# Two attention layers on one core: in the first layer, the fourth row block's transposes one unit later, the double work and its loads moved by up to three units

## The chip, the cores and the metric

The kernel runs on one core of a Trainium2 chip. A core has a matmul engine (TensorE, PE in the profile; its weight loads are PEld), three engines for elementwise work (VectorE or DVE, ScalarE or ACT, GpSimd or POOL) and SyncE (SP), which here issues nearly all DMA transfers. Each engine runs its own instructions in the order in which they were written, and waits at an instruction until what it needs is there. The metric is the time of one execution on the device in microseconds. Before the change it is 3582.98 us, the median of three runs (3582.79 to 3584.32).

## The reference

The input is one sequence of 2048 rows of width 640. Two kinds of block alternate, and the pair runs twice with the same weights:

```python
x = x + A(layernorm(x))   # attention, 32 heads of 20
x = x + B(layernorm(x))   # dense 640 -> 1536 -> 640 with relu squared
x = x + A(layernorm(x))
x = x + B(layernorm(x))

# A:
qkv = x @ wqkv                      # (2048, 640) @ (640, 1920)
p = softmax(q @ k.T * 20 ** -0.5)   # per head, over all 2048 keys
out = (p @ v) @ wo
# B:
r = max(x @ w1 + b1, 0)
out = (r * r) @ w2 + b2
```

Everything is float32. The kernel splits each operand of the projections into a high and a low part of the matmul's float32r format and adds three products, so that little precision is lost.

## The kernel before

**Stages.** A layer (`layer`) is a projection stage (`qkv`), an attention stage (`attention`), and an output and dense stage. The first layer's projection stage takes the first 340 us or so. Only this stage is touched.

**Rows and preparation.** The 2048 rows are four row blocks, `tb` 0 to 3, of 512 rows. Before a block can be projected, the generator `front` has to load its four row tiles, take their statistics (DVE, lines 244 and 245, and two small POOL operations), normalise them (DVE, line 252), transpose them on PE (line 469, in two groups of 12 and 8) and evict the result in high and low parts into five tiles `xnT`. For blocks 2 and 3 the eviction is a copy (ACT, L263), a rounding cast (ACT, L264) and a subtraction (POOL, L271). A `yield` ends each piece; `wait` holds two numbers of empty pieces, one ahead of the statistics, one ahead of the transposes. `fronts` chains the generators of blocks 1 to 3; `begin_first` builds them.

**Units.** The queries and keys are ten column groups of 128, `pos` 0 to 9. A unit is one column group for one row block: 15 matmuls of 512 columns into one PSUM bank. The list `UNITS` has 40: units 0 to 15 take the first four column groups (`FIRST`) block by block, units 16 to 39 the other six, four blocks each. Units 8 to 11 belong to block 2, units 12 to 15 to block 3. From unit 4 on, a matmul runs as two halves of 64 rows (L356 and L368), the second 19 matmuls behind the first (`LAG`). After each unit its bank is evicted and the result stored to DRAM; a store is issued some 16 steps after the unit's end. Sixteen value units (`v_unit`) follow the 40.

**Maxima.** Softmax needs the largest score of each query. The stage finds a part of them beside the projections, because DVE is the slowest at it. A *double* handles two chunks of 512 keys, `c` and `c + 1`, in one item: `step_two` multiplies the queries with the difference of the chunks (`kd`, tile "d" or "e") and ACT takes its Relu (L695); `both_two` multiplies them with chunk `c`, and DVE adds the two and takes the maximum (L702). Both matmuls are at L662. An item such as `(0, 0, "d")` (head group 0, query block 0) has eight pairs, that is 16 calls; the stage has 24 items, 384 calls. `tiles` loads what an item needs, if it isn't there: keys, difference keys and queries, six transfers each. When an item begins, the tiles of the next two are asked for as well.

**Order.** `between` is called after every matmul of a unit. It subtracts the matmul's cost (1, in a value unit 0.65) from a pace; when the pace is used up, it makes one call of the double work and adds 1.94. It issues stores that are due. Every third call in the first layer advances the preparation by one piece (`next(rest)`). `LATE_STEPS` says after which unit of the first layer tiles are loaded and doubles released. Calls that are left when the value units are over are made in a row:

```python
        while double or twos or begun:
            some()
```

**Buffers.** `xnT`, evicted units, weights, keys and queries share 42 slots of SBUF; row tiles and scratch tiles share 11; transposes and doubles take turns in five PSUM banks (`ps_q`), the units in three (`ps_pj`).

Of the kernel before, what the change touches and what calls it, by code (L numbers as in the profile page):

```python
# [39 lines left out]
def tile_layers(  # L40
# [26 lines left out]
    def slot(shape, dtype, label):  # L67
        return arena.tile(shape, dtype, tag="slot", name=name(label))

    def dma(eng, dst, src):  # L70

        if dst.dtype == F32R:
            dst = dst.bitcast(F32)
        if src.dtype == F32R:
            src = src.bitcast(F32)
        eng.dma_start(dst, src)  # L76
# [17 lines left out]
    ps_q = Ring(0, 1, 2, 3, 4)  # L94
# [20 lines left out]
    x_in = a_x[0]  # L115
# [92 lines left out]
    def raw_cols(src, j):  # L208
        raw = xtile("raw")
        dma(nc.sync, raw.rearrange("p (k m) -> p k m", k=KD),  # L210
            src[:, j * P : (j + 1) * P].rearrange("(k p) m -> p k m", p=P),
        )
        return raw
# [25 lines left out]
    def stats(x):  # L239

        st = small.tile([P, 2, 6], F32, tag="bst", bufs=3, name=name("bst"))
        mv = small.tile([P, 2], F32, tag="mv", bufs=6, name=name("mv"))
        for i in range(2):
            nc.vector.bn_stats(st[:, i, :], x[:, i * HALF : (i + 1) * HALF])
        nc.vector.bn_aggr(mv, st)
        var = mv[:, 1:2]
        nc.gpsimd.tensor_tensor(var, var, eps_t, op=ALU.add)
        nc.gpsimd.tensor_tensor(var, var, half_t, op=ALU.pow)
        return mv

    def normalise(eng, x, mv):
        eng.tensor_scalar(x, x, mv[:, 0:1], mv[:, 1:2], op0=ALU.subtract, op1=ALU.mult)  # L252

    def split_to(dst_hi, dst_lo, src):

        nc.scalar.copy(dst_hi, src)
        nc.vector.tensor_sub(dst_lo, src, dst_hi.bitcast(F32))  # L257

    def split_on_pool(dst_hi, dst_lo, src, r=None, hi=None):

        if r is None:
            r = xtile("r")[:, :QB]
        nc.scalar.copy(r, src)  # L263
        (hi or pool_hi)(dst_hi, r)  # L264
        pool_lo(dst_lo, r, dst_hi.bitcast(F32))
# [59 lines left out]
    def row_tile(src, r):  # L325
        t = xtile("x")
        dma(nc.sync, t, src[r * P : (r + 1) * P, :])
        return t
# [120 lines left out]
    def front(tb, x_src, bank, wait=(1, 1)):  # L449

        rows = [row_tile(x_src, tb * 4 + i) for i in range(4)]
        for _ in range(wait[0]):
            yield
        mvs = []
        for x in rows:
            mvs.append(stats(x))
            yield
        yield
        for x, mv in zip(rows, mvs):
            normalise(nc.vector, x, mv)  # L460
            yield
        for _ in range(wait[1]):
            yield
        res = []
        for ks in (range(3), range(3, KD)):
            dsts = [bank("xt") for _ in ks]
            for k, dst in zip(ks, dsts):
                for i in range(4):
                    nc.tensor.transpose(  # L469
                        dst[:, i * P : (i + 1) * P], rows[i][:, k * P : (k + 1) * P], ident  # L470
                    )
            for k, dst in zip(ks, dsts):
                t = slot([P, 2, QB], F32R, "xnT")
                if tb > 1:
                    split_on_pool(t[:, 0, :], t[:, 1, :], dst, None, nc.scalar.copy)
                else:
                    split_to(t[:, 0, :], t[:, 1, :], dst)
                res.append(t)
            if len(res) == KD:
                xt_[tb] = res  # L480
            yield
# [6 lines left out]
    def first_front(x_src):  # L488


        rows = [row_tile(x_src, i) for i in range(4)]
        yield
        mvs, dsts = [], [ps_all("xt") for _ in range(KD)]

        def turn(i):
            normalise(nc.vector, rows[i], mvs[i])
            for k in range(KD):
                nc.tensor.transpose(
                    dsts[k][:, i * P : (i + 1) * P], rows[i][:, k * P : (k + 1) * P], ident
                )  # L500
            warm(6 if i == 3 else 3)

        warm(11)
        for i in range(4):
            mvs.append(stats(rows[i]))
            if i:
                turn(i - 1)
            yield
        turn(3)
        yield  # L510
        res = []
        for dst in dsts:
            t = slot([P, 2, QB], F32R, "xnT")
            split_to(t[:, 0, :], t[:, 1, :], dst)
            res.append(t)
            if len(res) == KD:
                xt_[0] = res
            yield

    def fronts(steps):  # L520


        for n, f in enumerate(steps):
            for m, _ in enumerate(f):
                if m == 8 and n + 1 < len(steps):
                    next(steps[n + 1])
                yield
# [311 lines left out]
    def prep_job():  # L839
# [44 lines left out]
        19: [("double", 3)],  # L884
    }
    LATE_STEPS = {
        3: [("tiles", (0, 0, 0))],
        9: [("tiles", (0, 0, "d"))],
        11: [("double", 0), ("tiles", (1, 0, "d"))],
        13: [("double", 1)],  # L890
        16: [("double", 2)],
        19: [("double", 3)],
    }
# [507 lines left out]
    def begin_first():  # L1401
        f = first_front(x_in)
        next(f)
        for pos in range(FIRST):
            raws.append(raw_cols(wqkv, ORDER[pos]))
        for p in range(2):
            dma(nc.sync, d_one[:, p, :], ones)
        steps = [front(tb, x_in, ps_q, (4, 2)) for tb in (1, 2, 3)]
        for _ in range(5):
            next(f)  # L1410
        for pos in range(2):
            w_qk.put(
                raws.pop(0), pos * 10, pos * 10 + KD, KD, nc.scalar.copy,
                nc.vector.tensor_sub if pos else pool_lo,
            )
        next(steps[0])
        yield from f
        w_qk.put(raws.pop(0), 20, 20 + KD, KD, nc.scalar.copy, pool_lo)
        yield from fronts(steps)

    ones = slot([2, QB], F32, "ones")
    nc.vector.memset(ones, 1.0)
    ahead = second()
    layer(True, x_in, d_x[0], d_x[1], begin_first(), ahead)
    layer(False, d_x[1], d_x[2], x_out, ahead, None)

# [27 lines left out]
```

## Time and profile before

| | |
|---|---|
| median of three runs | 3582.98 us |
| profiled execution | 3582.95 us, its span 3581.2 us |
| mean granted PE clock | 0.998 |
| first projection stage | 0 to about 340 us |
| second projection stage | about 1800 to 2118 us |
| DMA over the span | 121 GB/s |

The profile lists the busy time of each engine, what each engine waited for, and the granted clock of PE, where 1.00 is full speed. Its lines start with a time in microseconds from the start of the span and a length. A bracket at the end is the idle time of the engine ahead of the instruction, with what ended it. A busy PE isn't PE at its peak: an instruction that is stretched by a lower clock counts as busy.

### The profile page before, as it was taken

The page shows a single profiled execution, that of the slowest core. Times are in us where ns is not written, and L with a number is a line of the kernel's source. Part 1 is how long each engine was busy: PE and PEld are TensorE (multiplying, and loading weights), DVE is VectorE, ACT ScalarE, POOL GpSimd, SP SyncE. Part 2 cuts the span into 40 slices and gives each one's busy share as a digit, 9 for nine tenths or more (in the row PEclk, how much of TensorE's full clock was granted, in tenths as well). Part 3 has the DMA queues.
Part 4 walks back from the last instruction along what each step waited for, and adds up shares of the span by engine and source line. Part 5 has one row for each costly group of instructions (what it writes and reads, how often), then busy time and mean ns, then how long its engine had stood idle before and what let it go on. Part 6 is the DMA issues. An engine that isn't in the chain of part 4 may idle for free.

```text
span 3581.2 us, 70902 instructions
## 1 busy us (share of the span) xinstructions
PE 3558.4 (99%) x25544; PEld 2153.0 (60%) x25544; DVE 2630.3 (73%) x5078; ACT 2708.6 (76%) x4730; POOL 832.4 (23%) x939
## 2 busy tenths in 40 slices
PE   9999999999999999999999999999999999999999
PEld 7998333333333336988989973333333333378998
DVE  6999888888888881444579988888888888725443
ACT  5888999999999995122238889999999999932221
POOL 5430334322112211112243201212112211201110
PEclk9999999999999999999999999999999999999999
DMA  7666455422222136722356652222232121375221
GB/s 239 220 219 193 136 161 153 148 73 70 59 56 57 47 106 199 259 74 74 103 190 223 197 176 67 79 73 60 69 84 57 42 60 51 108 239 208 75 81 37
DMA packets 281598, 431.87 MB, mean 121 GB/s; under 512 B 70948, under 2 KB 130084, under 8 KB 281248
## 3 DMA queue, kind: packets, MB, share of 16 engines
q1 hardware_dynamic: 280720, 425.64, 38.2%
q8 instruction: 203, 3.33, 0.4%
q10 hardware_dynamic: 528, 1.70, 0.2%
q14 instruction: 147, 1.20, 0.1%
HBM read 282.52 MB, written 144.68 MB: 119 GB/s over the span
## 4 chain that ended last, share of the span: by engine, by line
PE 94%; DVE 2%; ACT 1%; DMA 1%; issue 1%; POOL 1%; SPq 0%; ACTq 0%; POOLq 0%; DVEq 0%
PE banks L771 27%; PE banks L336 21%; PE banks L756 18%; PE banks L662 17%; PE banks L368 5%; PE banks L356 5%; PE banks L351 1%; ACT e L766 0%; PE banks L469 0%; DMA x<-d_x 0%; SPq L76 0%; DVE h L257 0%; DVE r L1302 0%; ACT r L1301 0%; DVE x L252 0%
## 5 line engine op out<-in xcount | busy, mean ns | idle before, releaser
L766 ACT ACTIVATE e<-banks 128x512 f32<-128x512 f32 (+1 forms) x3416 | 2037.7, 690 | 52.9 <-PE banks L756 12.7
L673 DVE TENSOR_REDUCE mx<-banks 128x1 f32<-128x512 f32 x2560 | 1620.3, 685 | 323.1 <-PE banks L662 275.4
L771 PE MATMUL banks<-e,vg 128*32 128x512 f32 x8192 | 1094.3, 605 | 2.3 <-ACT e L766 2.3
L662 PE MATMUL banks<-k,q 60*128 60x512 f32 x3360 | 1056.5, 411 | 0.5 <-DVE mx L702 0.4
L756 PE MATMUL banks<-q,k 62*128 62x512 f32 x4096 | 1049.9, 442 | 1.0
L756 PEld LDWEIGHTS banks<-q,k 62*128 62x128 f32 x4096 | 515.7, 185 | 751.3 <-ACT e L766 494.0
L662 PEld LDWEIGHTS banks<-k,q 60*128 60x128 f32 x3360 | 564.9, 185 | 196.6 <-ACT e L766 65.0
L702 DVE CUSTOM_DVE_ANT_0 rl<-banks,rl 128x512 f32<-128x512 f32 x736 | 476.5, 689 | 52.0 <-PE banks L662 28.8
L695 ACT ACTIVATE rl<-banks 128x512 f32<-128x512 f32 x736 | 399.1, 601 | 58.5 <-PE banks L662 49.5
L771 PEld LDWEIGHTS banks<-e,vg 128*32 128x32 f32 x8192 | 162.2, 108 | 353.7 <-issue 269.3
L1301 ACT ACTIVATE r<-banks,b_t 128x512 f32<-128x512 f32 x96 | 66.2, 689 | 377.9 <-PE banks L336 227.3
L336 PE MATMUL banks<-w,h 128*128 128x320 f32 x2304 | 348.9, 310 | 2.7 <-DVE h L257 2.5
L336 PEld LDWEIGHTS banks<-w,h 128*128 128x128 f32 x2304 | 339.2, 188 | 11.4 <-DVE h L257 6.4
L336 PE MATMUL banks<-xnT,w 128*128 128x512 f32 x1440 | 329.7, 389 | 0.0
L368 PE MATMUL banks<-xnT,wqk 64*128 64x512 f32 x1080 | 326.1, 393 | 0.0
L356 PE MATMUL banks<-xnT,wqk 64*128 64x512 f32 x1080 | 325.6, 394 | 0.0
L336 PEld LDWEIGHTS banks<-xnT,w 128*128 128x128 f32 x1440 | 269.5, 188 | 55.3
L815 POOL TENSOR_TENSOR few<-few,minus_t 128x16 f32<-128x16 f32 x62 | 179.9, 2902 | 228.9 <-DMA few<-d_s 228.8
L662 PE MATMUL banks<-kd,q 60*128 60x512 f32 x736 | 208.3, 399 | 2.8 <-ACT rl L695 2.4
L268 POOL CAST mr<-nt 128x32 fp32r<-128x32 f32 x64 | 13.5, 211 | 835.8 <-DVE nt L728 835.8
L356 PEld LDWEIGHTS banks<-xnT,wqk 64*128 64x128 f32 x1080 | 199.7, 187 | 11.4 <-issue 2.0
L368 PEld LDWEIGHTS banks<-xnT,wqk 64*128 64x128 f32 x1080 | 201.5, 187 | 7.6
(93 smaller groups left out, 2731.7 us busy)
## 6 DMA issues: line engine op xcount, KB each, us to landing
q<-d_qk SPq DMA_DIRECT2D x876, 80.0 KB
d_qk<-ev SPq DMA_DIRECT2D x80, 512.0 KB
k<-d_qk SPq DMA_DIRECT2D x444, 80.0 KB
x<-d_x SPq DMA_DIRECT2D x96, 320.0 KB
d_o<-ot SPq DMA_DIRECT2D x248, 80.0 KB
ot<-d_o SPq DMA_DIRECT2D x38, 512.0 KB
d_v<-v SPq DMA_DIRECT2D x32, 512.0 KB
vg<-d_v SPq DMA_DIRECT2D x32, 512.0 KB
```

Source lines behind the costliest of these rows:

```text
L336: nc.tensor.matmul(dst, a, b, start=(n == 0), stop=(n == last))
L356: top = nc.tensor.matmul(dst, a[:64], b[:64], start=start, stop=last)
L368: low = nc.tensor.matmul(dst, a, b, start=False, stop=last, skip_group_check=True)
L662: nc.tensor.matmul(dst, q_t[t][b : b + 60, p, sub * P : (sub + 1) * P], k_t[t // NQB, c][b : b + 60, p, :], start=True, stop=True,)
L673: nc.vector.tensor_reduce(maxima(t)[:, 2 * p + par, sub, c : c + 1], dst, axis=AX.X, op=ALU.max)
L695: nc.scalar.activation(r, dst, AF.Relu)
L702: nc.vector.tensor_tensor_reduce(out=r[par], in0=dst, in1=r[par], scale=1.0, scalar=LEAST, op0=ALU.add, op1=ALU.max, accum_out=maxima(t)[: ...
L756: nc.tensor.matmul(dst, k_t[t // NQB, kt // 4][b : b + 62, p, (kt % 4) * P : (kt % 4 + 1) * P], q_t[t][b : b + 62, p, :], start=True, stop ...
L766: nc.scalar.activation(dst, src, AF.Exp, scale=SCALE)
L771: nc.tensor.matmul(acc[32 * h : 32 * h + 32, :], v_t[t // NQB, kt // 8][:, kt % 8, 32 * h : 32 * h + 32], es[p][:, par, :], start=(kt == 0 ...
L815: nc.gpsimd.tensor_tensor(few, few, minus_t, op=ALU.pow)
L1301: nc.scalar.activation(r, dst, AF.Relu, bias=b1_t[:, f : f + 1])
```

## The change

Three places change, all for the first layer's projection stage.

- `front` of block 3 gets seven empty pieces ahead of its transposes in place of two. Five pieces are 15 calls of `between`, one unit.
- The keys of chunk 0 and the queries of item (0, 0) are loaded after unit 6, not after unit 3; the difference keys of group 0 after unit 8, not after unit 9.
- The first two doubles are released after unit 10, not 11, together with the loads of group 1's first item; the next four after unit 12, not 13. The later releases, after units 16 and 19, stay.

```diff
     LATE_STEPS = {
-        3: [("tiles", (0, 0, 0))],
-        9: [("tiles", (0, 0, "d"))],
-        11: [("double", 0), ("tiles", (1, 0, "d"))],
-        13: [("double", 1)],
+        6: [("tiles", (0, 0, 0))],
+        8: [("tiles", (0, 0, "d"))],
+        10: [("double", 0), ("tiles", (1, 0, "d"))],
+        12: [("double", 1)],
         16: [("double", 2)],
         19: [("double", 3)],
     }
...
-        steps = [front(tb, x_in, ps_q, (4, 2)) for tb in (1, 2, 3)]
+        steps = [front(tb, x_in, ps_q, (4, 7 if tb == 3 else 2)) for tb in (1, 2, 3)]
```

## The prediction

> **What bounds the kernel now.** I read the page first, then the waits of the matmul engine (PE) alone, then stretches of time, then the order of work inside the two stretches that fell short.
>
> ```profile
> span 3581.2 us, 70902 instructions
> PE 3558.4 (99%) x25544; PEld 2153.0 (60%) x25544; DVE 2630.3 (73%) x5078; ACT 2708.6 (76%) x4730; POOL 832.4 (23%) x939
> ```
>
> PE idles 22.8 us in all, so a change of order can win only there, or where PE is busy at half clock. The waits (total, times, longest) name the place:
>
> ```profile
> PE banks L469 <- DVE x L252: 5.0, 4, 2.9
> PE banks L662 <- ACT rl L695: 2.4, 8, 0.4
> PE banks L662 <- DVE mx L702: 0.4, 1, 0.4
> ```
>
> L469 is the transposes of a row block, L252 the normalising in front of them. The stretches around the longest wait (busy us of PE, PEld, DVE, ACT, POOL; then the granted clock, DMA share, GB/s):
>
> ```profile
> 54.00:56.00 2.00, 0.33 (x1) 0.14 (x1) 2.00 (x3) 0.00 (x0) 2.00 (x2) 1.00 0.00 0
> 56.00:58.00 2.00, 0.88 (x3) 0.59 (x4) 1.61 (x3) 0.00 (x0) 0.67 (x1) 0.64 0.94 358
> 58.00:60.00 2.00, 2.00 (x11) 1.67 (x11) 0.00 (x0) 1.78 (x4) 0.53 (x1) 0.50 0.81 261
> 62.00:64.00 2.00, 2.00 (x12) 1.59 (x12) 0.00 (x0) 1.48 (x3) 1.41 (x2) 0.65 1.09 254
> ```
>
> PE starves from 52 to 57 us and is then granted half its clock until about 63.4 (0.65 is 1.4 us at a half and 0.6 at full). The order inside, start and length in us:
>
> ```profile
> 38.29 1.53 PE L469 MATMUL banks<-ident,x 128*128 128x128 f32 x12
> 40.65 1.09 PE L469 MATMUL banks<-ident,x 128*128 128x128 f32 x8
> 45.20 0.39 PE L356 MATMUL banks<-xnT,wqk 64*128 64x512 f32 x1
> ...
> 51.78 0.39 PE L356 MATMUL banks<-xnT,wqk 64*128 64x512 f32 x1
> 52.34 0.33 PE L469 MATMUL banks<-ident,x 128*128 128x128 f32 x1 [0.18 <-DVE x L252]
> 55.60 0.33 PE L469 MATMUL banks<-ident,x 128*128 128x128 f32 x1 [2.93 <-DVE x L252]
> 57.07 2.70 PE L469 MATMUL banks<-ident,x 128*128 128x128 f32 x10 [1.14 <-DVE x L252]
> 61.28 1.97 PE L469 MATMUL banks<-ident,x 128*128 128x128 f32 x8
> 71.81 0.41 PE L662 MATMUL banks<-kd,q 60*128 60x512 f32 x2
> ```
>
> The first two rows are the third block's 12 and 8 transposes, unhindered. The next two are 29 steps apart, so a projection step takes 0.227 us. The fourth block's transposes follow: one, a gap, one, a gap, ten, and eight from 61.28 on. The last row is the first double.
>
> **What the change moves.** Every projection step calls the pacing function once, every third call advances the preparation, a unit has 15 steps. Five more waiting turns are 15 steps: the fourth block's transposes go from steps 141 and 144 to 156 and 159, one unit or 15 x 0.227 = 3.4 us of other matmuls. Nothing ahead of them on VectorE (DVE), ScalarE (ACT) or GpSimd (POOL) moves.
>
> **Idle before the transposes.** What DVE and POOL do meanwhile:
>
> ```profile
> L252 DVE TENSOR_SCALAR x<-x,mv x4: 559/1076/1553, 51.7 to 56.9; 128x640 f32<-128x640 f32 x4
> 53.99 3.55 DVE L252 TENSOR_SCALAR x<-x,mv 128x640 f32<-128x640 f32 x3
> 53.73 2.94 POOL L271 TENSOR_TENSOR ev<-r,ev 128x512 fp32r<-128x512 f32 x2
> 49.70 1.30 POOL L271 TENSOR_TENSOR ev<-r,ev 128x512 fp32r<-128x512 f32 x1
> 51.81 0.59 ACT L263 COPY r<-banks 128x512 f32<-128x512 f32 x1 [2.16 <-POOL mv L248]
> 52.43 0.62 ACT L264 CAST ev<-r 128x512 fp32r<-128x512 f32 x1
> ```
>
> A normalising takes 0.56 us alone and 1.55 us beside a POOL subtraction. The rows' tiles are ready at 52.3, 55.5, 57.0 and 57.5. With the change PE arrives at 52.2 + 3.4 = 55.6: rows 0 and 1 are there, and it waits 1.2 us for row 2 and 0.4 for row 3. But unit 8's end now comes before this, 15 steps after unit 7's (evicted from 51.81 on), so its copy and cast end at about 51.81 + 1.2 + 3.4 = 56.4, and POOL, free at 56.67, starts a third subtraction just ahead of the last normalising. If that blocks it like the two before, row 3 comes at 58.5 and the second gap is 1.2 us. Idle before: 0.18 + 2.93 + 1.14 = 4.25. After: 1.6 (not blocked) to 2.4 (blocked). I take the middle, 2.0: **gain 2.25** (bounds 0, if all gaps move along, and 2.65). [...]
>
> **Half clock.** From 57.07 to 63.25 PE did 10 transposes, 3 steps and 8 transposes in 6.18 us. At full clock these take 10/12 x 1.53 + 0.68 + 1.09 = 3.05. The drop cost 3.1 us. If the smaller gaps no longer trigger it, **gain 3.1** (bounds 0 and 3.1; the case of 0 is the first rival).
>
> **The doubles, one unit sooner.** Their work on PE is the same; what changes is what they meet. ACT evicts the transposes:
>
> ```profile
> 58.16 0.59 ACT L263 COPY r<-banks 128x512 f32<-128x512 f32 x1 [5.11 <-PE banks L469]
> 59.30 0.58 ACT L263 COPY r<-banks 128x512 f32<-128x512 f32 x1
> 76.05 0.50 PE L662 MATMUL banks<-kd,q 60*128 60x512 f32 x1 [0.33 <-ACT rl L695]
> 83.27 1.01 PE L662 MATMUL banks<-kd,q 60*128 60x512 f32 x2
> ```
>
> One bank costs ACT 1.14 us (59.30 - 58.16). Before, 37 steps lay between the last transposes and the first double; now it is 8, or 1.8 us. With transposes from 58.0, group one ends at 59.2 and group two at 60.9; ACT, at five times 1.14 from 58.3, ends at 64.0, while the first double comes at 62.7. Its two Relus and unit 9's eviction queue behind; the third double needs their banks (five in the ring) and PE waits about 1.9 us, in place of 0.33 in the row at 76.05: **cost 1.6** (bounds 0 and 3.1, ACT's whole lead). The doubles also meet one more unit of those that ACT evicts with two passes: of the 2.4 us that PE waits for L695, spread over four such units, a fifth adds **0.5** (bounds 0 and 1).
>
> **The loads.** SyncE issues in order and waits there:
>
> ```profile
> 31.97 2.98 SPq L76 DMA_DIRECT2D q<-d_qk  x6
> 45.83 0.38 SPq L76 DMA_DIRECT2D d_qk<-ev  x1
> 60.37 8.53 SPq L76 DMA_DIRECT2D d_qk<-ev  x2
> 68.95 2.68 SPq L76 DMA_DIRECT2D kd<-d_kd  x6
> 74.71 4.94 SPq L76 DMA_DIRECT2D q<-d_qk  x12
> ```
>
> Keys and queries of group 0 (12 issues near 0.45 us) leave their place before 35 us and stand behind unit 4's stores, so from 48.2 to 53.6. Units 5 to 7's stores and the difference keys of (0,0) follow, done near 58.3, and those keys land by 60, ahead of 62.7. The next 24 loads (group 1 and the queries of (0,1)) now stand ahead of unit 8's store, whose wait for POOL held them until 68.95. They run from about 60 to 70.5, and the last lands 4 us later, at 74.5; 16 doubles and 30 steps after 62.7 they are needed at about 75 with the wait above. Before, PE lost half a microsecond there (1.01 for a pair that takes 0.41). Unit 8's store is 2 us later and nobody soon reads it: **0**, bounds a gain of 0.5 and a loss of 1.
>
> **The end of the stage.** The doubles are 384 calls. A step pays 1 and a value step 0.65 into a pace of 1.94, so before there were (420 + 480 x 0.65) / 1.94 = 377.3 turns: 378 calls, and 6 were left to run bare, each waiting for DVE. With 15 more steps it is 385: none is left. The second layer shows what the hand-over looks like with none left:
>
> ```profile
> 336.72 2.50 PE L368 MATMUL banks<-wv,xnT 64*128 64x320 f32 x16
> 350.66 1.06 PE L771 MATMUL banks<-e,vg 128*32 128x512 f32 x8
> 2115.85 2.80 PE L368 MATMUL banks<-wv,xnT 64*128 64x320 f32 x18
> 2123.96 1.07 PE L771 MATMUL banks<-e,vg 128*32 128x512 f32 x8
> 343.00:344.00 1.00, 0.89 (x2) 0.40 (x2) 1.00 (x3) 0.53 (x1) 0.00 (x0) 0.65 0.93 373
> 350.00:351.00 1.00, 1.00 (x9) 0.37 (x9) 0.70 (x2) 1.00 (x3) 0.00 (x0) 0.94 0.69 152
> 84.75 0.23 PE banks L662 x2
> ```
>
> From the trailing half matmuls to the second group of value products, the first layer takes 13.94 us (with the clock at a half from 343.3 to 350.1), the second 8.11. Of the 5.83 more, six calls at 0.23 are 1.4 that PE must do anyway, in unit 11 now. **Gain 4.4** (bounds 2.5, if the clock still drops there, and 5).
>
> **Sum.** 2.25 + 3.1 - 1.6 - 0.5 + 4.4 = 7.65 us. The profiled execution took 3582.95 (span 3581.2 and 1.75 around it), 0.03 under the median of 3582.98, so the sum gives 3575.3. Attention and everything behind keep their order.
>
> **Rivals.** (1) *The half clock comes back.* For it: the drop at 343.3 followed a stretch in which PE still worked, and the two new gaps lie within 2.9 us. Against: they are 1.2 and at most 1.2 us, where 2.93 stood. Its 3.1 us are then lost, but PE reaches the doubles when ACT has caught up, so the 1.6 falls away, and 0.3 of the old wait too: 7.65 - 3.1 + 1.6 + 0.3 = 6.4, or 3576.5; with the blocked normalising 3576.9. Within 0.2% (7.2 us, about what a measurement of this kernel can tell from no change). [...] (2) *The hand-over gives less*, because something else (the last value tiles, a clock drop of its own) holds attention: gain 2.5 there, 5.75 in all, 3577.2. (3) *Slower: late loads.* If the 24 loads still start near 68.95, for instance because a buffer comes free only then, the queries of (0,1) land at 83.8 as before, against a need at 75: 9 us of idle PE and a clock drop of 3.4 turn 7.65 into a loss of 4.8. It decides from a landing at 79 on, and passes 0.2% from about 86. Against it: unit 8's store, which held them, now stands behind them. (4) The change does nothing: the transposes wait as long, one unit later, and only the hand-over gains: 3578.5.
>
> **How the numbers follow.** Forecast, more than 0.2% faster: 0.55. Rival 1: 0.18, rival 2: 0.07, rival 4: 0.06, all within 0.2%, together 0.31. Rival 3 and its like beyond 0.2%: 0.14. The forecast's range goes to 3572.5 (no wait for ACT, unblocked row 3, the longer hand-over gain). Upward 3581.0 takes in rivals 1, 2 and 4 and a part of 3; slower than that I leave out.
>
> **What would show it.** Right: L469 <- L252 near 3 us in total, longest under 1.5; granted clock 1.00 from 56 to 64 and from 343 to 350; no L662 between the last trailing half matmul and the first L756; value products some 7.6 us earlier. Wrong: a clock of 0.50 after the transposes (rival 1); L662 waiting long for L695 near 65 us, or on a q tile near 75 (rival 3); the first L771 later than 6 us behind the trailing halves (rival 2).

## The result, and the profile after

The changed kernel took 3577.14 us (median of 14 runs, 3575.85 to 3580.10) against 3583.47 for the kernel before (14 runs, 3580.53 to 3588.13). The ratio is 0.9982, with a 95% interval of 0.9974 to 0.9990: faster by 6.3 us. The forecast was 3575.3, in a range of 3572.5 to 3581.0. It gave a chance of 0.55 to a gain of more than 0.2% (7.2 us); the median gain, 0.18%, falls just short of that, where the forecast had put 0.31, and the interval, 0.10% to 0.26%, takes in both. The two profiled executions stand further apart, 3582.95 and 3575.89, or 7.1 us: the one of the changed kernel is the second fastest of its 14, 1.25 us under their median. Nine of the 14 runs show a mean clock of 1.000 and a median of 3576.82, the five at 0.999 one of 3579.91. The mean is too coarse to count single drops (the profiled execution of kernel 9 below reads 1.000 with 3.4 us at half clock in it), so how many of the 14 have a drop isn't known.

The page of the changed kernel, then the waits of PE over its whole span (total, times, longest):

```profile
span 3574.1 us, 70896 instructions
PE 3553.5 (99%) x25544; PEld 2147.6 (60%) x25544; DVE 2632.1 (74%) x5078; ACT 2707.3 (76%) x4730; POOL 832.2 (23%) x939
...
PE banks L469 <- DVE x L252: 3.0, 3, 1.1
PE banks L662 <- ACT rl L695: 2.6, 5, 1.1
...
PE banks L662 <- DMA q<-d_qk: 0.6, 1, 0.6
```

The transposes' wait fell from 5.0 us to 3.0, its longest from 2.9 to 1.1. The longest wait for ScalarE's Relu grew from 0.4 to 1.1, and a wait for queries from DRAM is new. The same stretches as before the change, with the clock third from the right:

```profile
56.00:58.00 2.00, 0.33 (x1) 0.14 (x1) 2.00 (x2) 0.44 (x1) 2.00 (x2) 1.00 0.72 243
58.00:60.00 2.00, 1.38 (x11) 1.22 (x13) 0.63 (x2) 0.93 (x2) 0.21 (x1) 1.00 1.01 298
62.00:64.00 2.00, 2.00 (x20) 1.65 (x18) 0.00 (x0) 1.97 (x4) 2.00 (x2) 1.00 1.07 369
...
343.00:344.00 1.00, 1.00 (x9) 0.20 (x9) 1.00 (x3) 1.00 (x3) 0.00 (x0) 1.00 0.88 260
```

PE still idles, but the clock stays at full speed in both places. The timeline of PE, with the last rows from the hand-over:

```profile
55.54 0.46 PE L469 MATMUL banks<-ident,x 128*128 128x128 f32 x2
57.14 0.33 PE L469 MATMUL banks<-ident,x 128*128 128x128 f32 x1 [1.15 <-DVE x L252]
58.62 1.20 PE L469 MATMUL banks<-ident,x 128*128 128x128 f32 x9 [1.15 <-DVE x L252]
60.64 1.09 PE L469 MATMUL banks<-ident,x 128*128 128x128 f32 x8
63.61 0.40 PE L662 MATMUL banks<-kd,q 60*128 60x512 f32 x2
67.48 0.50 PE L662 MATMUL banks<-kd,q 60*128 60x512 f32 x1 [1.12 <-ACT rl L695]
77.45 0.47 PE L662 MATMUL banks<-kd,q 60*128 60x512 f32 x1 [0.65 <-DMA q<-d_qk]
...
335.18 2.80 PE L368 MATMUL banks<-wv,xnT 64*128 64x320 f32 x18
343.30 1.07 PE L771 MATMUL banks<-e,vg 128*32 128x512 f32 x8
```

A ledger of the stage comes from these rows and those of the kernel before. The transposes' stretch ended at 63.25 us and now ends at 61.73, with 15 more steps (3.4 us) in it: 4.9 us gained. From there to the trailing halves it took 273.47 us and now takes 273.45, though 3.4 us of steps left that stretch and six calls (1.4 us) came in: 2.0 lost. From the trailing halves to the second group of value products it took 13.94 and now takes 8.12, of which 1.4 is the moved calls: 4.4 gained. The sum is 7.3 us at the second value group (343.30 against 350.66).

### The profile page after: what moved, and what is told of

The parts are those of the page before. It is cut to its first block, busy times and chain, and to the rows that moved or that the text cites. A ratio compares the mean times of both kernels' runs of the same rounds, so it can differ in the third digit from the quotient of the medians.

```text
span 3574.1 us, 70896 instructions
## 1 busy us (share of the span) xinstructions
PE 3553.5 (99%) x25544; PEld 2147.6 (60%) x25544; DVE 2632.1 (74%) x5078; ACT 2707.3 (76%) x4730; POOL 832.2 (23%) x939
## 4 chain that ended last, share of the span: by engine, by line
PE 95%; DMA 1%; ACT 1%; DVE 1%; POOL 1%; issue 0%; SPq 0%; ACTq 0%; POOLq 0%; DVEq 0%
PE banks L771 28%; PE banks L336 22%; PE banks L756 18%; PE banks L662 17%; PE banks L368 5%; PE banks L356 5%; PE banks L351 1%; SPq L76 0%; ACT e L766 0%; PE banks L469 0%; DVE h L257 0%; DVE r L1302 0%; ACT r L1301 0%; DVE x L252 0%; ACT h L256 0%
## 5 line engine op out<-in xcount | busy, mean ns | idle before, releaser
L695 ACT ACTIVATE rl<-banks 128x512 f32<-128x512 f32 x736 | 398.9, 601 | 56.6 <-PE banks L662 46.6
```

The lines of the kernel that those rows point to most:

```text
L695: nc.scalar.activation(r, dst, AF.Relu)
```

## The experiments

The third column is the start of the third group of value products in the first layer's attention, an end mark of the stage that the trace of one execution gives. Kernels 1 to 4, 5 to 7 and 9, and 8, 10 and 11 ran with their own runs of the kernel before.

| | ratio to before | difference of medians, us | third group at, us |
|---|---|---|---|
| before | | | 352.78 |
| changed kernel | 0.9982 (0.9974 to 0.9990) | -6.3 | 345.43 |
| 1 transposes only | 0.9989 (0.9981 to 0.9998) | -3.6 | 350.58 |
| 2 loads and doubles only | 0.9987 (0.9978 to 0.9995) | -5.0 | 348.18 |
| 3 pace only | 0.9989 (0.9981 to 0.9998) | -3.7 | 349.13 |
| 4 transposes and pace | 0.9982 (0.9973 to 0.9991) | -6.3 | 345.29 |
| 5 six calls left again | 0.9991 (0.9982 to 0.9999) | -3.5 | 349.26 |
| 6 first loads as before | 0.9983 (0.9975 to 0.9992) | -6.3 | 346.60 |
| 7 low part on VectorE | 0.9983 (0.9974 to 0.9992) | -5.5 | 345.94 |
| 8 transposes 24 steps later, pace | 0.9981 (0.9972 to 0.9990) | -7.3 | 344.99 |
| 9 transposes 6 steps later | 0.9983 (0.9974 to 0.9992) | -5.8 | 346.32 |
| 10 as 8, thinner pace | 0.9977 (0.9968 to 0.9985) | -8.1 | 345.83 |
| 11 transposes 21 steps later | 0.9984 (0.9975 to 0.9993) | -6.0 | 345.57 |

The intervals are some 6 us wide, so the times don't show differences of 1 us between kernels. The traces show where one execution of each spent its time, but a difference of 1 us in the third column is no proof either: the execution kept of the changed kernel is 1.25 us under its median, that of kernel 1 is the slowest of its 11 (1.6 us above the median), that of kernel 6 is 0.9 us above.

**1. The transposes alone.**

```diff
-        steps = [front(tb, x_in, ps_q, (4, 2)) for tb in (1, 2, 3)]
+        steps = [front(tb, x_in, ps_q, (4, 7 if tb == 3 else 2)) for tb in (1, 2, 3)]
```

> Only the fourth block's transposes move by one unit; loads, doubles and pace stay as before, so six calls of the double work are again left at the stage's end. My theory: the transposes' idle time falls from 4.25 us to 2.3 and the half clock after them is gone (3.1 us), so 5.0 us less than before, the doubles' start at step 180 finds ScalarE free, and the clock still drops behind the stage's end near 340 us. Rival, the hand-over carries the whole gain: 0 to 2 us less than before, with the clock at a half after the transposes.

It gained 3.6 us, between the two theories. The gaps are those of the changed kernel, but in this execution the clock fell behind them:

```profile
57.42 0.33 PE L469 MATMUL banks<-ident,x 128*128 128x128 f32 x1 [1.15 <-DVE x L252]
58.90 1.72 PE L469 MATMUL banks<-ident,x 128*128 128x128 f32 x9 [1.15 <-DVE x L252]
62.12 1.42 PE L469 MATMUL banks<-ident,x 128*128 128x128 f32 x8
...
58.00:60.00 2.00, 1.10 (x8) 1.10 (x9) 0.92 (x2) 0.65 (x2) 0.49 (x1) 0.86 0.89 279
60.00:62.00 2.00, 2.00 (x9) 1.04 (x7) 0.00 (x0) 1.97 (x4) 1.37 (x2) 0.50 0.67 176
62.00:64.00 2.00, 2.00 (x14) 1.67 (x14) 0.00 (x0) 1.56 (x4) 2.00 (x2) 0.79 0.98 175
...
333.14 2.50 PE L368 MATMUL banks<-wv,xnT 64*128 64x320 f32 x16
347.49 1.93 PE L771 MATMUL banks<-e,vg 128*32 128x512 f32 x8
```

From the row at 58.90 to the end of the last one pass 4.64 us, against 3.11 in the changed kernel: a drop costs 1.5 us here, where it cost 3.1 before, because it lasts 3.4 us (59.4 to 62.8) and not 6.8. The same gaps went with a drop in kernels 1 and 5, and with none in the changed kernel and kernels 4 and 6. Kernel 5 differs from the changed kernel on PE only from its first double at 65.09 us on, behind the gaps. So rival 1 is a matter of the execution, and neither theory of the prediction is right for all.

At the trailing halves this execution is 3.6 us ahead of the kernel before (333.14 against 336.72). At the third group it is 2.2 ahead: the half clock of the hand-over lasted 10.2 us here (339.3 to 349.6) and 6.8 before, so the price of the hand-over differs between executions too.

**2. The loads and the doubles alone.**

```diff
-        steps = [front(tb, x_in, ps_q, (4, 7 if tb == 3 else 2)) for tb in (1, 2, 3)]
+        steps = [front(tb, x_in, ps_q, (4, 2)) for tb in (1, 2, 3)]
```

(against the changed kernel)

> Only the loads and the release of the doubles move; the transposes stay where they were. My theory: the 2.93 us wait and the half clock at 57 to 63 us stay, no call is left at the end, the hand-over gains 4.4 us and one more unit of crowded ScalarE costs 0.5: 3.9 us less than before. Rival, the transposes carry the whole gain: no change or a loss near 1 us. Rival, the loads in their new places hold the doubles: a wait for a q or kd tile of more than 1 us between 65 and 80 us.

It gained 5.0 us, 4.6 at the third group. PE's timeline shows the old gap and the new hand-over together:

```profile
55.56 0.33 PE L469 MATMUL banks<-ident,x 128*128 128x128 f32 x1 [2.93 <-DVE x L252]
57.03 2.71 PE L469 MATMUL banks<-ident,x 128*128 128x128 f32 x10 [1.14 <-DVE x L252]
...
337.94 2.80 PE L368 MATMUL banks<-wv,xnT 64*128 64x320 f32 x18
346.05 1.06 PE L771 MATMUL banks<-e,vg 128*32 128x512 f32 x8
```

The trailing halves come 1.2 us later than before (336.72), and the calls that moved ahead of them are worth 1.4. So the doubles one unit sooner cost nothing where the transposes stay in place (the wait for L695 is 0.69 us at 71.48, 0.33 at 76.05 in the kernel before), and the 0.5 us that was expected for a crowded unit didn't appear. Neither rival shows.

**3 and 5. The hand-over, from both sides.** The pace sets how many calls are left, without moving anything by hand:

```diff
-    DOUBLE_PACE = {False: 1.97, True: 1.94}
+    DOUBLE_PACE = {False: 1.97, True: 1.90}     # 3: on the kernel before
+    DOUBLE_PACE = {False: 1.97, True: 1.975}    # 5: on the changed kernel
```

> The kernel before with the first layer's pace for a double call at 1.90 in place of 1.94: (420 + 480 x 0.65) / 1.90 = 385 turns, so no call is left at the end, and nothing else moves. My theory, that the bare calls and the clock drop behind them cost 4.4 us: 4.4 us less than before, less whatever the denser calls cost on VectorE (it is busy 97% there, so up to 2 us). Rival, the hand-over is slow for another reason (the first layer's loads, the last value tiles): the value products start no earlier, no change.

> The changed kernel with the pace at 1.975 in place of 1.94: (435 + 480 x 0.65) / 1.975 = 378 turns, so six calls are again left bare at the stage's end, while transposes, loads and doubles stay moved. My theory (the hand-over is 4.4 us of the gain, because no call is left): 4.4 us more than the changed kernel, less about 1 us for thinner calls (the pace of 1.90 cost the kernel before 1.1 us of its stage), so 3 to 4.5 us more, with the clock at a half behind 340 us again. Rival, the hand-over is faster because everything came earlier: no more than 1 us over the changed kernel.

The kernel before without bare calls gained 3.7 us; the changed kernel with six lost 2.9 of its 6.3, and 3.8 at the third group. The hand-over of kernel 3, then that of kernel 5:

```profile
338.88 2.80 PE L368 MATMUL banks<-wv,xnT 64*128 64x320 f32 x18
347.00 1.06 PE L771 MATMUL banks<-e,vg 128*32 128x512 f32 x8
```

```profile
333.04 2.80 PE L368 MATMUL banks<-wv,xnT 64*128 64x320 f32 x18
337.10 0.50 PE L662 MATMUL banks<-k,q 60*128 60x512 f32 x1 [0.35 <-DVE mx L702]
347.12 1.06 PE L771 MATMUL banks<-e,vg 128*32 128x512 f32 x8
```

Without bare calls it is 8.12 us, as in the changed kernel; with six it is 14.08, as before (13.94). Net of the six calls' own 1.4 us, bare calls cost 4.4 us in the kernel before and 4.6 in kernel 5, and 8.1 us is what the changed kernel and kernels 2 and 3 show without them. That calls left over cause the price is shown. Kernel 1, also with six, took 14.35 us and lost another 1.4 by the third group to its longer half clock. Most of the price is likely the clock: 6.8 us at half clock are up to 3.4 us lost, by an estimate. The denser pace of kernel 3 costs 0.8 us of its stage (338.88 - 336.72, less the 1.4 of the calls).

**4. Transposes late, doubles in their old place.** Experiment 1's edit together with experiment 3's.

> The kernel before with the transposes one unit later and the pace at 1.90; doubles and loads stay in their old places. My theory: both gains without the price of the doubles' early start (1.6 us of waiting for ScalarE, 0.5 for one more crowded unit): 9.4 us less than before, 2 to 3 us under the changed kernel, less up to 2 us for the denser calls. Rival, the early doubles are what makes the gain: no better than the transposes alone, 5 us.

It gained 6.3 us, not 9.4. Here the doubles start at 66.79 us, behind ScalarE's evictions, and the 1.1 us wait is gone, yet the third group comes only 0.1 us earlier than in the changed kernel. Part of what the early start costs comes back in the pace of 1.90 (0.8 us by kernel 3), 0.47 us is a wait for the queries of (0, 1) at 79.10, and the rest wasn't traced. That the early doubles make the gain isn't shown either, since this kernel reaches the same without them.

**6. The first loads in their old places.**

```diff
-        6: [("tiles", (0, 0, 0))],
-        8: [("tiles", (0, 0, "d"))],
+        3: [("tiles", (0, 0, 0))],
+        9: [("tiles", (0, 0, "d"))],
```

> The changed kernel with the first item's keys and queries loaded after unit 3 and its difference keys after unit 9, as before; doubles, their other loads and transposes stay moved. My theory, the place of these loads is worth nothing because SyncE is idle enough either way: within 0.7 us of the changed kernel, and the 0.65 us wait for a q tile at 77 us stays or shrinks. Rival, the later loads are part of the gain (they take DMA out of the crowded 28 to 44 us) or a part of the price (they delay stores): 1 us or more either way.

The times say no difference, the trace says 1.2 us at the third group. PE's timeline has two waits for loads:

```profile
64.76 0.47 PE L662 MATMUL banks<-kd,q 60*128 60x512 f32 x1 [0.53 <-DMA kd<-d_kd]
78.80 0.47 PE L662 MATMUL banks<-kd,q 60*128 60x512 f32 x1 [2.13 <-DMA q<-d_qk]
```

With early doubles the difference keys are needed one unit sooner too, and the wait for queries is 2.13 us where it was 0.65, though SyncE has issued these queries only 0.3 us later (74.30 against 73.99); why they land so late wasn't traced. My theory of no effect isn't borne out by the trace. Whether 1 us is left of it in the time stays open.

**7. What blocks the last normalising.**

```diff
-            split_on_pool(ev[:, 0, :], ev[:, 1, :], dst, r, nc.scalar.copy)
+            if plan["late"] and tb == 2 and jj == 0:
+                nc.scalar.copy(r, dst)
+                nc.scalar.copy(ev[:, 0, :], r)
+                nc.vector.tensor_sub(ev[:, 1, :], r, ev[:, 0, :].bitcast(F32))
+            else:
+                split_on_pool(ev[:, 0, :], ev[:, 1, :], dst, r, nc.scalar.copy)
```

> The changed kernel with one instruction moved: the low part of unit 8's keys is subtracted on VectorE, behind the last normalising, not on GpSimd ahead of it (its copy goes into a scratch tile and not into the keys' tile, so the difference keys of block 2 are not what the reference needs; the time is read for the order alone). My theory, GpSimd's subtraction blocks the last normalising: it ends near 57.6 us and not 58.5, the second gap before the transposes falls from 1.15 to about 0.2 us, and the kernel is up to 1 us faster. Rival, the normalising is slow for another reason: the second gap stays at 1.15.

(The expectation errs in its bracket: for this block `r` is the keys' tile, so nothing of the computation is left out.) The changed kernel's row for the normalising and for GpSimd's subtraction, then rows of kernel 7, whose transposes are at L474 and doubles at L667:

```profile
L252 DVE TENSOR_SCALAR x<-x,mv x4: 560/1553/1578, 51.8 to 57.0; 128x640 f32<-128x640 f32 x4
56.70 1.51 POOL L271 TENSOR_TENSOR ev<-kf,ev 128x512 fp32r<-128x512 f32 x1
```

```profile
L252 DVE TENSOR_SCALAR x<-x,mv x4: 559/1078/1579, 51.7 to 57.0; 128x640 f32<-128x640 f32 x4
57.64 1.20 PE L474 MATMUL banks<-ident,x 128*128 128x128 f32 x9 [0.20 <-DVE x L252]
76.22 0.46 PE L667 MATMUL banks<-kd,q 60*128 60x512 f32 x1 [0.84 <-DVE mx L707]
78.13 0.47 PE L667 MATMUL banks<-kd,q 60*128 60x512 f32 x1 [1.44 <-DMA q<-d_qk]
```

Three of four normalisings took 1.55 us in the changed kernel, two in kernel 7, and the gap fell from 1.15 to 0.20. So the subtraction blocks the normalising (1.55 us beside one, 0.56 without), shown. Yet nothing was won: PE is 1 us ahead behind the transposes, then waits 0.84 us for VectorE at 76 us and 0.8 longer than before for the queries of (0, 1) at 78 us. Those two are the next limits in this trace.

**9 and 11. Six and 21 steps in place of 15.**

```diff
-(4, 7 if tb == 3 else 2)
+(4, 4 if tb == 3 else 2)     # 9
+(4, 9 if tb == 3 else 2)     # 11
```

> The changed kernel with the transposes six steps later than before in place of fifteen. My theory: PE comes 1.36 us later than in the kernel before and 2.04 earlier than in the changed one, in front of a last normalising that nothing blocks (unit 8's end is behind the transposes), so idle 4.25 - 1.36 = 2.9 us, ScalarE 9 steps more ahead of the doubles (the 1.1 us wait for L695 near 67 us goes), the hand-over as in the changed kernel: 0 to 1 us more than the changed kernel if the clock holds, 3 us more if it falls. Rival, the wait for ScalarE weighs more than the gaps: faster than the changed kernel.

> The changed kernel with the transposes 21 steps later in place of 15, the doubles still released after unit 10. My theory, gaps and ScalarE's queue are one chain (last normalising, five evictions, first Relus): the gaps fall from 2.3 us to about 1.2, but the doubles now start two steps behind the transposes, and the wait for L695 near 67 us grows by as much: within 0.7 us of the changed kernel. Rival, the gaps count by themselves: 1 us faster than the changed kernel.

Kernel 9 idled 3.1 us in its gaps, had a drop of the clock from 59.0 to 62.4 and a wait of 0.76 for L695, and ended 0.9 us behind the changed kernel at the third group, where 3 us had been expected with a drop. Kernel 11 is the clearer one:

```profile
58.54 1.20 PE L469 MATMUL banks<-ident,x 128*128 128x128 f32 x9 [1.14 <-DVE x L252]
65.29 0.50 PE L662 MATMUL banks<-k,q 60*128 60x512 f32 x1 [0.65 <-ACT rl L695]
67.40 0.50 PE L662 MATMUL banks<-kd,q 60*128 60x512 f32 x1 [1.12 <-ACT rl L695]
```

One gap of two is gone, and a second wait for ScalarE stands in its place; the third group is 0.1 us later. Last normalising, five evictions and first Relus are one chain, and PE waits for it in one place or the other.

**8 and 10. Later transposes, doubles in their old place.**

```diff
-(4, 2)) for tb in (1, 2, 3)]
+(4, 10 if tb == 3 else 2)) for tb in (1, 2, 3)]
...
-    DOUBLE_PACE = {False: 1.97, True: 1.94}
+    DOUBLE_PACE = {False: 1.97, True: 1.90}     # 8
+    DOUBLE_PACE = {False: 1.97, True: 1.92}     # 10
```

> The kernel before with the transposes 24 steps later in place of 15 (eight waiting pieces more), doubles and loads in their old places, the pace at 1.90. My theory: PE reaches the transposes near 57.6 us and waits only for the last row's normalising, about 1 us in place of 2.3, no drop of the clock in any execution, the doubles at step 181 stand 13 steps behind the transposes and wait little for L695: 1 to 1.5 us under the kernel with 15 steps and a pace of 1.90, near 3575. Rival, ScalarE's eviction of the transposes now runs into the doubles and takes it back: no gain over that kernel, with a wait for L695 over 1 us near 66 us.

> The same with the pace at 1.92: (420 + 480 x 0.65) / 1.92 = 381 turns, so 2 calls are left bare. My theory: the thinner calls give back half of the 1.1 us that 1.90 cost, and two bare calls cost 0.5 to 1.5 us with no drop of the clock: within 1 us of the kernel with 1.90. Rival, any bare call brings the whole slow hand-over: 3 to 4 us more, with the clock at a half near 340 us.

Kernel 8, near 59 and 66 us:

```profile
58.92 1.20 PE L469 MATMUL banks<-ident,x 128*128 128x128 f32 x9 [0.53 <-DVE x L252]
65.67 0.50 PE L356 MATMUL banks<-xnT,wqk 64*128 64x512 f32 x1 [0.68 <-ACT r L263]
```

Its idle time at the transposes is 0.53 us, where kernel 4 had 2.3, and it gained 7.3. Against kernel 4 that is 0.7 us by the medians and 0.3 at the third group, less than the 1 to 1.5 expected: PE now waits 0.68 us for ScalarE and 0.57 for the queries at 78.86. Kernel 10 has the best median, 3575.05, 2 us under the changed kernel's, but the intervals overlap. Its two bare calls still brought a half clock (0.50 from 340 to 342 us), which had not been expected, for a hand-over of 10.62 us (333.09 to 343.71), 2.0 more than 8.12 and the two calls' own 0.5; its third group is 0.8 us behind kernel 8's, so the trace doesn't explain the better median, and which pace is best stays open.

## Why the prediction was right

The time lay in the range, and each step can be set beside a row of the one profiled execution. The steps as measured there sum to 1.95 + 3.0 - 2.0 + 4.4 = 7.35 us against 7.65. The medians give 6.3; what the usual execution loses against the one kept isn't shown.

- **Idle before the transposes**: 4.25 us fell to 2.3 (two gaps of 1.15). The step took 2.0, the middle between blocked and not; the blocked end, 2.4, is what came, and experiment 7 shows why. Gain 1.95 in place of 2.25.
- **Half clock**: gone in the profiled execution, 3.0 us where 3.1 were taken. But experiments 1 and 5 have the same gaps with a drop. The choice between the forecast and rival 1 was put as one or the other; it is both, by execution, and that the kept execution is without the drop is luck. Such drops may be what puts the median behind that execution; this isn't shown.
- **The doubles sooner**: 1.6 for ScalarE's lead and 0.5 for a crowded unit were 2.1 together, measured 2.0. The split was wrong, and the agreement is luck: experiment 2 shows no price for the crowded unit, the wait for ScalarE is 1.12 us where 1.9 was worked out (0.8 more than the 0.33 before, not 1.6), 0.65 is a wait for a load, and about half a microsecond wasn't traced.
- **The loads**: the keys and queries of (0, 0) came in time, as worked out (12 issues from 48.28 on). The next 24 loads didn't start at 60. They start at 63.78, because the first of them reads what unit 6's store, issued at 58.41, has yet to write. SyncE's own waits and rows:

```profile
58.41 0.38 SPq L76 DMA_DIRECT2D d_kd<-kd  x1
63.78 2.75 SPq L76 DMA_DIRECT2D kd<-d_kd  x6
SPq L76 <- DMA d_kd<-kd: 3.0, 1, 3.0
```

That dependence was missed. Rival 3 has its place here, at 0.65 us and not at 9. That the later start makes these 0.65 us isn't shown: in kernel 6 the 24 loads start at 61.28, and its wait is longer.
- **The hand-over**: 4.4 us taken, 4.4 measured, and confirmed by taking it away and by adding it alone. Reading the price from the second layer's hand-over was the best step of the forecast.

Rivals 2 and 4 are excluded: the hand-over is the second layer's (8.12 against 8.11), and the transposes alone gain 3.6 us. Rival 3 came only as the 0.65 us above, and the clock stayed at 1.00 there (74 to 86 us), so of the drop of 3.4 us that it had added nothing came. The last normalising was blocked: three of the four took 1.55 us, where 0.56 is the time without a subtraction beside it.

## What to carry to other kernels

Where PE is 99% busy, look at the few waits that are left and at what follows them: here the drop of the clock behind the wait was worth more (3.0 us) than the idle time that went (1.95). Work that is spread by a pace should run out just before its stage does; six calls left over cost 4.4 us, and a stage that hands over well elsewhere in the same trace gives the price. When a wait is moved, follow its chain to the end: here the normalising, the evictions, the Relus and then a load took turns at the front, and closing one gap alone won nothing.

## What had not been expected of the hardware

The clock fell behind the same two gaps of 1.15 us in two executions of five. Added up from stretches of 0.1 us, the half clock (0.50) lasted 3.41 us behind these gaps (from 59.43 us in experiment 1), 6.83 us behind the gaps of the kernel before (from 56.58) and 10.24 us at experiment 1's hand-over (from 339.32): one, two and three times the same length. The two drops of one execution begin 279.89 us apart in experiments 1 and 5 (59.70 and 339.59 in the latter) and 286.72 us apart in the kernel before (56.58 and 343.29), 82 and 84 times a third of that 10.24. That is what these three executions show; that it holds in others isn't shown.

The 3.41 us ahead of the drops weren't idle throughout: PE was busy for 0.10 of them in the kernel before, for 0.33 and 0.36 in experiments 1 and 5, and for 0.80 or 0.81 ahead of the hand-overs. The busy share alone doesn't decide: in kernel 9, 3.41 us with PE busy for 0.51 of them (52.2 to 55.6) led to no drop, and the next, at 0.57 (55.6 to 59.0), did. In experiments 1 and 5 the 3.41 us ahead of the drop held both gaps almost whole. What makes the clock fall behind the same gaps in one execution and not in another isn't shown.
